# Moving work between VectorE, GpSimd and ScalarE in the spectral stage of a fused block, with reordered loads

## The chip, the cores and the metric

The kernel runs on one NeuronCore of a Trainium2 chip. The metric is the device time of one execution in microseconds (us). Every run is of one core.

Engine names as the profile prints them: PE is TensorE (matmuls), PEld its weight loads, DVE is VectorE, ACT is ScalarE, POOL is GpSimd, SP is the engine that issues DMAs.

## The reference

A block with layer norm and modulation, a spectral filter, and a gated feed-forward part:

```
mod = (silu(c) @ w_mod)                     # six rows: sa, ca, ga, sb, cb, gb
h = layernorm(x) * (1 + ca) + sa            # x: 2048 x 640, bf16
X = rfft2(h) * (w_r + 1j * w_i)             # filter in the frequency domain
x = x + ga * irfft2(X)
h = layernorm(x) * (1 + cb) + sb
x = x + gb * ((silu(h @ w_gate) * (h @ w_up)) @ w_down)    # 640 -> 1728 -> 640
```

The kernel computes the Fourier transforms as matmuls with tables.

## The kernel before

There are four stages. The *front* transforms the rows (to about 40 us). The *spectral middle* walks through 21 groups of at most four spectral lines: transform, multiply with the filter, transform back. The *inverse stage* makes the 16 output tiles of the filter and the second layer norm. The *feed-forward part* takes the remaining two thirds.

Line numbers below are those of the kernel named; the change shifts them, so the product line is L490 before and L496 after.

One group in the middle goes through three functions, and all engines work on neighbouring groups at the same time.

```python
def stage_a(g):                                     # TensorE, then VectorE
    for i, l in enumerate(ls):
        nc.tensor.matmul(xps[:, i, 0:192], lhsT=B2[:, j, :], rhs=KS2, ...)      # L476
        # (last ten groups: five one-column matmuls for the modulation, L480)
    for hl in range(2):                             # two products with the filter
        nc.vector.tensor_tensor(PP[:, 1:4, hl], xv[:, :, hl], in1, ALU.mult)    # L490
    nc.vector.tensor_copy(PP[:, 0], PP[:, 1])       # L491: the first plane again

def stage_b(g, PP):                                 # 8 matmuls, then an evacuation
    nc.tensor.matmul(yps[:, i, :], lhsT=_rev(PP, ...), rhs=identb[:], ...)      # L499
    nc.scalar.copy(Y2[:, 0:n, :], yps[:, 0:n, :])                               # L502

def stage_c(g, Y2):                                 # 4 matmuls, evacuation, rotation
    nc.tensor.matmul(eps_[:, i, :], lhsT=Y2[:, i, :], rhs=Ktab[...], ...)       # L511
    if g % 8 == 7:
        nc.vector.tensor_copy(Ev, ev)                                           # L526
    else:
        nc.scalar.copy(Ev, ev)                                                  # L528
    ...
    rot(l8, l0 + 4 - l8, slice(0, 64), nc.gpsimd)   # every second group: two ops

# in the loop over the groups:
    sa_add(g + 4)                                   # GpSimd adds a constant, four times
    if g in (0, 2):
        wsum(Wv, 16 * g, 16 * g + 32, nc.vector)    # weight sums
    if g in (9, 13):                                # "RI products": scale the RI table
        nc.gpsimd.tensor_tensor(RI[:, v], RI[:, v], ga_bc[:], ALU.mult)
# ... cut: the front, the inverse stage, the feed-forward part
```

The input `B2` of groups 5 to 20 arrives by four DMA transposes. The RI table is loaded between the second and the third of them. The gate and up weights are loaded in two pieces (columns 0 to 511, then 512 to 1663), both ahead of the DMA transpose that brings the first normalized chunk to the feed-forward part.

## Time and profile before

Median 278.97 us of 4 runs (278.12 to 279.92). The profiled execution has a span of 276.7 us.

| stage | from, us | to, us | what holds it |
|---|---|---|---|
| front | 0 | 41.77, first product | several engines |
| middle | 41.77 | 71.01, end of the last product | VectorE |
| tail of the middle | 71.01 | 74.32, first burst of inverse matmuls | a chain over three engines |
| inverse stage | 74.32 | 93.63 | TensorE |
| feed-forward | 93.63 | 276.7 | TensorE |

The page of the profile names what held the end (part 4, "chain that ended last"). The shares are of the whole span:

```profile
PE 78%; DVE 9%; DMA 5%; ACT 3%; SPq 1%; issue 1%; POOL 0%; DVEq 0%; ACTq 0%
PE psum L714 20%; PE psum L717 20%; PE psum L759 19%; DVE rM L490 3%; DMA rL<-rA 3%; DMA rW<-rL 2%; PE psum L265 2%; PE psum L313 2%; PE psum L650 2%; PE psum L665 2%; PE psum L287 2%; PE psum L284 1%; DVE rM L491 1%; PE psum L704 1%; PE psum L668 1%; PE psum L303 1%
```

L714, L717 and L759 are the feed-forward part, which the change leaves alone. The 9% of VectorE are mostly the middle. The chain also passes through a DMA transpose there (`rL<-rA`, the third of the four). It did not hold the stage: it landed at 55.92 us, while VectorE was busy all along, and the first matmul that reads it started at 57.73 us, after a wait for VectorE:

```profile
46.59 9.34 DMA rL<-rA
```

```profile
57.73 0.24 PE L476 MATMUL psum<-Ktab,rL 128*128 128x192 bf16 x1 [0.54 <-DVE rM L490]
```

In the middle the groups of instructions (window 41 to 71 us) show how full VectorE is. The columns are line, engine, operation, output and input, shapes, count; busy us and mean ns of one; idle us of the engine just before them and who ended that.

```profile
L490 DVE TENSOR_TENSOR rM<-psum,rW 128x384 bf16<-128x384 f32 (+2 forms) x42 | 21.0, 539 | 0.6 <-PE psum L476 0.6
L499 PE MATMUL psum<-identb,rM 128*128 128x128 bf16 x154 | 12.4, 220 | 1.0 <-DVE rM L490 0.5 <-DVE rM L491 0.4
...
L491 DVE COPY rM<-rM 128x256 bf16<-128x256 bf16 (+2 forms) x20 | 6.8, 340 | 0.7
...
L540 POOL TENSOR_SCALAR rE<-rE 128x512 bf16<-128x512 bf16 (+1 forms) x8 | 5.0, 626 | 11.2 <-ACT rE L528 9.7 <-DVE rE L526 1.4
```

The products wait 0.6 us in all, which is their first wait, at 41.77 us. VectorE never stops after it. GpSimd stands still for 11.2 us before its rotations (L540).

Next the timeline of VectorE in the same stage: start us, duration us, engine, line, operation. "x2" merges two instructions.

```profile
60.39 0.35 DVE L491 COPY rM<-rM 128x256 bf16<-128x256 bf16 x1
60.65 1.01 DVE L490 TENSOR_TENSOR rM<-psum,rW 128x384 bf16<-128x384 f32 x2
61.70 1.18 DVE L491 COPY rM<-rM 128x256 bf16<-128x256 bf16 x1
62.79 1.01 DVE L490 TENSOR_TENSOR rM<-psum,rW 128x384 bf16<-128x384 f32 x2
63.84 0.23 DVE L491 COPY rM<-rM 128x256 bf16<-128x256 bf16 x1
```

The same copy takes 0.23 us at 63.84 and 1.18 us at 61.70. GpSimd at that moment:

```profile
60.04 0.62 POOL L540 TENSOR_SCALAR rE<-rE 128x512 bf16<-128x512 bf16 x1 [1.30 <-ACT rE L528]
...
61.38 1.40 POOL L574 TENSOR_TENSOR rH<-rH,ga_bc 128x640 bf16<-128x640 bf16 x1
```

The 1.18 us copy starts in the shadow of a 1.40 us RI product on GpSimd, and it ends at 62.88 us, just after that product (62.79 us). Where the timelines of both engines were read (this kernel, the copies alone on GpSimd, and parts of the two weight sum runs), each of the eleven copies on VectorE that took more than 0.30 us, 0.35 to 1.23 us long, ended 0.04 to 0.08 us after an operation of GpSimd. By these ends the copy was held until GpSimd was done, rather than slowed; "stretched" means this below. Not every operation held one: at 51.08 us a copy kept its 0.23 us and ended while a 0.31 us add ran on GpSimd. The products of VectorE do not change their pace (1.01 or 1.02 us for each merged pair of full size in this kernel, whatever GpSimd does).

### The profile page before, as it was taken

To read this page: it belongs to the slowest core of one execution; us is meant where nothing else is said; L and a number is where in the kernel's file an instruction comes from. 1 tells how busy PE (TensorE), PEld (TensorE's weight loads), DVE (VectorE), ACT (ScalarE), POOL (GpSimd) and SP (SyncE) were. 2 spreads that over 40 slices of the span, in tenths; PEclk is the share of its full clock that TensorE was granted. 3 is DMA by queue.
4 is the path that set the end of the run, shared out by engine and by line. 5 is a ranking of instruction groups with operands and counts; after the bars stand their busy time and mean duration, and the time that the engine had idled before them with its cause. 6 is when DMAs were issued, how large, how long until landed. Compare 5 with 4: busy or idle time off the path is not lost.

```text
span 276.7 us, 5481 instructions
## 1 busy us (share of the span) xinstructions
PE 263.9 (95%) x2202; PEld 179.3 (65%) x2202; DVE 153.9 (56%) x371; ACT 111.6 (40%) x206; POOL 46.7 (17%) x90
## 2 busy tenths in 40 slices
PE   8899989888799999999999999999999999999995
PEld 3688768787589887644446754445764444778873
DVE  0577969999688789338634227654223633323422
ACT  2588657876777772143222022323004223103310
POOL 4277742474410002000200000200000100000000
PEclk9999999999999999999999999999999999999999
DMA  7999999999993000610050110050011020011001
GB/s 243 370 301 287 325 353 205 303 285 368 241 388 78 7 1 0 121 33 1 2 95 0 50 56 1 0 96 1 24 51 33 0 50 0 25 35 43 1 2 47
DMA packets 40952, 31.30 MB, mean 113 GB/s; under 512 B 20831, under 2 KB 37342, under 8 KB 40542
## 3 DMA queue, kind: packets, MB, share of 16 engines
q1 hardware_dynamic: 40924, 30.94, 38.6%
q8 instruction: 17, 0.28, 0.4%
q14 instruction: 9, 0.07, 0.1%
q10 hardware_dynamic: 2, 0.00, 0.0%
HBM read 23.37 MB, written 4.72 MB: 101 GB/s over the span
## 4 chain that ended last, share of the span: by engine, by line
PE 78%; DVE 9%; DMA 5%; ACT 3%; SPq 1%; issue 1%; POOL 0%; DVEq 0%; ACTq 0%
PE psum L714 20%; PE psum L717 20%; PE psum L759 19%; DVE rM L490 3%; DMA rL<-rA 3%; DMA rW<-rL 2%; PE psum L265 2%; PE psum L313 2%; PE psum L650 2%; PE psum L665 2%; PE psum L287 2%; PE psum L284 1%; DVE rM L491 1%; PE psum L704 1%; PE psum L668 1%; PE psum L303 1%
## 5 line engine op out<-in xcount | busy, mean ns | idle before, releaser
L714 PE MATMUL psum<-rW 128*128 128x512 bf16 (+1 forms) x325 | 66.9, 336 | 0.0
L717 PE MATMUL psum<-rW 128*128 128x512 bf16 (+1 forms) x325 | 66.9, 336 | 0.0
L720 ACT ACTIVATE rE<-psum 128x512 f32<-128x512 f32 (+1 forms) x65 | 33.3, 512 | 68.4 <-PE psum L714 68.3
L717 PEld LDWEIGHTS <-rW 128*128 128x128 bf16 x325 | 31.8, 98 | 24.5
L714 PEld LDWEIGHTS <-rW 128*128 128x128 bf16 x325 | 31.8, 98 | 24.5
L721 DVE TENSOR_TENSOR rX<-psum,rE 128x512 bf16<-128x512 f32 x26 | 17.9, 688 | 30.0 <-PE psum L717 28.5
L764 DVE TENSOR_TENSOR rE<-psum,rM 128x640 bf16<-128x640 f32 x15 | 12.4, 824 | 38.3 <-PE psum L759 38.3
L721 DVE TENSOR_TENSOR rE<-psum,rE 128x256 bf16<-128x256 f32 (+1 forms) x39 | 19.9, 511 | 24.6 <-PE psum L717 22.6
L759 PE MATMUL psum<-rA,rE 128*128 128x320 bf16 x224 | 31.2, 299 | 0.7 <-DVE rA L727 0.6
L759 PE MATMUL psum<-rA,rX 128*128 128x320 bf16 x224 | 30.8, 299 | 0.0
L759 PEld LDWEIGHTS <-rE 128*128 128x128 bf16 x224 | 21.9, 98 | 9.6 <-issue 0.6
L759 PEld LDWEIGHTS <-rX 128*128 128x128 bf16 x224 | 21.9, 98 | 8.8
L623 POOL TENSOR_TENSOR rstd<-rstd,mhalf 128x4 f32<-128x4 f32 (+1 forms) x5 | 4.4, 885 | 136.6 <-DVE rstd L619 107.3
L706 ACT ACTIVATE rE<-psum 64x512 f32<-64x512 f32 (+1 forms) x5 | 2.5, 506 | 48.1 <-PE psum L704 48.1
L490 DVE TENSOR_TENSOR rM<-psum,rW 128x384 bf16<-128x384 f32 (+2 forms) x42 | 21.0, 539 | 0.6 <-PE psum L476 0.6
L337 DVE SCALAR_TENSOR_TENSOR rE<-rE,msum,psum 128x648 bf16<-128x648 f32 x16 | 14.2, 889 | 4.1 <-PE psum L287 3.6
L502 ACT CAST rL<-psum 128x512 bf16<-128x512 f32 (+2 forms) x21 | 12.3, 586 | 7.3 <-PE psum L499 6.8
L670 DVE TENSOR_TENSOR rM<-psum,rX 128x640 f32<-128x640 f32 x16 | 12.9, 815 | 3.4 <-PE psum L668 3.4
L499 PE MATMUL psum<-identb,rM 128*128 128x128 bf16 x162 | 13.1, 220 | 1.3 <-DVE rM L490 0.8
L306 ACT COPY rE<-psum 128x640 bf16<-128x640 bf16 x16 | 10.9, 693 | 8.0 <-PE psum L304 8.0
L655 ACT CAST rL<-psum 128x640 bf16<-128x640 f32 x16 | 10.9, 690 | 4.6 <-PE psum L652 3.4
L352 ACT CAST rA<-psum 128x648 bf16<-128x648 f32 x15 | 10.5, 700 | 5.1 <-PE psum L349 3.9
(127 smaller groups left out, 361.7 us busy)
## 6 DMA issues: line engine op xcount, KB each, us to landing
rM<-in_w_mod_dram SPq DMA_DIRECT2D x4, 800.0 KB, 6.3
out_dram<-rE SPq DMA_DIRECT2D x16, 160.0 KB, 1.8
rA<-in_B_w_down_dram SPq DMA_DIRECT2D x1, 2080.0 KB, 13.2
rX<-in_A_x_dram SPq DMA_DIRECT2D x3, 640.0 KB, 8.2
rM<-in_w_mod_dram SPq DMA_DIRECT2D x1, 1600.0 KB, 7.9
rW<-in_B_w_gate_dram SPq DMA_DIRECT2D x1, 1440.0 KB
rW<-in_B_w_up_dram SPq DMA_DIRECT2D x1, 1440.0 KB, 13.5
rE<-tab_G SPq DMA_DIRECT2D x4, 256.0 KB, 8.4
```

The source lines that it names most:

```text
L306: nc.scalar.copy(hT[:, :, 0:128], xt)
L337: nc.vector.scalar_tensor_tensor(Z[:].rearrange("p (h r) n -> p h (r n)", h=2), Cb[:].rearrange("p (h r) n -> p h (r n)", h=2), msum[:, t: ...
L490: nc.vector.tensor_tensor(PP[:, 1:4, hl], xv[:, :, hl], in1, ALU.mult)
L499: nc.tensor.matmul(yps[:, i, :], lhsT=_rev(PP, 128 * n * ps + i, [[n, 128]]), rhs=identb[:], start=(ps == 1 and i == 0), stop=(ps == 0 and ...
L502: nc.scalar.copy(Y2[:, 0:n, :], yps[:, 0:n, :])
L670: nc.vector.tensor_tensor(x1[:, t, :].rearrange("p (m h r) -> p m h r", h=2, r=2), ops[:, :, 0:320].rearrange("p h (r m) -> p m h r", r=2) ...
L714: nc.tensor.matmul(gu[:, 0, 0:N], lhsT=Wgu[:, 0, c5, fc * 128:(fc + 1) * 128], rhs=h2T[:, :, c5, :], start=(c5 == 0), stop=(c5 == NC5 - 1))
L717: nc.tensor.matmul(gu[:, 1, 0:N], lhsT=Wgu[:, 1, c5, fc * 128:(fc + 1) * 128], rhs=h2T[:, :, c5, :], start=(c5 == 0), stop=(c5 == NC5 - 1))
L720: nc.scalar.activation(sg[:], gu[:, 0, 0:N], ACT.Silu)
L721: nc.vector.tensor_tensor(AT[:, fc, :], gu[:, 1, 0:N], sg[:], ALU.mult)
L759: nc.tensor.matmul(ops4[:, h, 0:320], lhsT=AT[:, fc, tl * 128:(tl + 1) * 128], rhs=Wd_sb[:, fc, h * 320:(h + 1) * 320], start=(fc == 0), s ...
L764: nc.vector.tensor_tensor(xo[:].rearrange("p (h m) -> p h m", h=2), ops4[:, :, 0:320], x1[:, t, :].rearrange("p (h m) -> p h m", h=2), ALU ...
```

## The change

Its intent is to spread the middle evenly over the engines. The core of the diff, with cuts:

```diff
-            nc.vector.tensor_copy(PP[:, 0], PP[:, 1])
+            if g % 4 == 0:
+                nc.vector.tensor_copy(PP[:, 0], PP[:, 1])
+            else:
+                nc.gpsimd.tensor_scalar(PP[:, 0], PP[:, 1], 1.0, 1.0, ALU.mult, ALU.mult)
...
-                nc.gpsimd.tensor_tensor(B2b[:, :nb, 0:1], B2b[:, :nb, 0:1], SA[...], ALU.add)
+                nc.vector.tensor_tensor(B2b[:, :nb, 0:1], B2b[:, :nb, 0:1], SA[...], ALU.add)
...
-            if g in (9, 13):
-                v = (g - 9) // 4
-                nc.gpsimd.tensor_tensor(RI[:, v], RI[:, v], ga_bc[:], ALU.mult)
+            if g + 3 == NG:
+                ...
+                for v in (1, 0):
+                    nc.vector.tensor_tensor(RI[:, v], RI[:, v], ga_bc[:], ALU.mult)
...
+            elif g < NG - 4:                  # two groups evacuated in one go
+                n = len(groups[g]) + 4
+                nc.scalar.copy(ep_views(l0, n), banks(6, 2, [8, 128])[:, 8 - n:8, :]...)
+                rot(l0, n, slice(0, 64), nc.gpsimd)
...
+            if slot == 0:                     # evacuation and constant in one operation
+                nc.vector.tensor_tensor(B2[:], tp[:, :n, :], SAx[:], ALU.add)
...
-        nc.sync.dma_start(RI[:], RI_dram)     # between the DMA transposes
         nc.sync.dma_start(wm_r[:, :, 1:3, :], wm_m[:, :, 1:3, :])
...
         nc.sync.dma_start(Htab[:], H_dram)
+        nc.sync.dma_start(RI[:], RI_dram)
...
-    for lo, hi in ((0, 512), (512, 1664)):
+    wgu_dma(0, 512)
+    wgu_dma(512, 1024)
...
             if t == 5:
                 ln2_tr(0)
+                wgu_dma(1024, 1664)           # behind the first chunk's transpose
```

Cut: the last four groups are evacuated and rotated in pieces by ScalarE and VectorE; two accumulations of the front use other PSUM banks; one weight sum of the front moves a tile earlier, the one of group 0 to before the loop and the one of group 2 to group 4; the last matmuls of a group are delayed so that two groups go together, and their input Y2 gets four buffers instead of two; the modulation rows are evacuated in another order.

More of the change, by code (lines that the diff above doesn't have):

```diff
@@ L177, in adaln_block_kernel @@
     SA = const.tile([P, NL], F32, name="SA")
+    SAx = gb_bc[:, 0:512].rearrange("p (l k) -> p l k", l=4)
     x_sb = rX.cut(0, [NT, D])
@@ L342, in s1 @@
         def s1(t, Z, Gs):
-            aps = banks(6, 2, [2, 512]) if t < NT - 1 else zbank(t - 1)
+            aps = banks(0 if t in (13, 15) else 6, 2, [2, 512])
             zr, zi = Z[:, :, 0:81], Z[:, :, 81:162]
@@ L369, in adaln_block_kernel @@
         nc.gpsimd.memset(SL[:], 0.0)
+        nc.gpsimd.memset(SAx[:], 0.0)
         nc.gpsimd.tensor_copy(sc_rep[:], sc_f[:].unsqueeze(2).to_broadcast([P, NC5, 128]))
@@ L399, in adaln_block_kernel @@
                 gscale(t)
-            if t in (9, 11, 13, 15):
-                wsum(Wn, 8 * t - 72, 8 * t - 56, nc.vector)
+            if t in (9, 11, 13, 14):
+                i = (9, 11, 13, 14).index(t)
+                wsum(Wn, 16 * i, 16 * i + 16, nc.vector)
             if t == NT - 1:
-                mps = psum[:, 0, 0:NC5]
+                mps = psum[:, 2, 480:480 + NC5]
                 mod_cols(mps, wm_sa, True)
@@ L409, in adaln_block_kernel @@
                                   src.unsqueeze(2).unsqueeze(3).to_broadcast([P, 4, 2, NT]))
-        sps = psum[:, 1, 0:NL]
+        sps = psum[:, 2, 0:NL]
         for i in range(16):
@@ L415, in adaln_block_kernel @@
         wsum(Wn, 64, 81, nc.vector)
+        nc.vector.tensor_scalar_mul(SAx[:, :, 0], sps[:, 64:68], float(P))
+        nc.vector.tensor_scalar_mul(SA[:], sps, float(P))
         wsum(Wv, 64, 81, nc.vector)
-        nc.vector.tensor_scalar_mul(SA[:], sps, float(P))
     Em = rE.cut(0, [2, 64, 128])
@@ L451, in t2_pe @@
             B2 = (rM.cut(38400 + 1024 * slot, [n, 128]) if slot < 2 else rM.cut(10240 + 1024 * (slot - 2), [n, 128]))
-            nc.scalar.copy(B2[:], tp[:, :n, :])
-            eng = nc.vector if slot == 0 else nc.gpsimd
-            eng.tensor_tensor(B2[:, 0:4, 0:1], B2[:, 0:4, 0:1], SA[:, ls[0]:ls[0] + 4].unsqueeze(2), ALU.add)
+            if slot == 0:
+                nc.vector.tensor_tensor(B2[:], tp[:, :n, :], SAx[:], ALU.add)
+            else:
+                nc.scalar.copy(B2[:], tp[:, :n, :])
+                nc.gpsimd.tensor_tensor(B2[:, 0:4, 0:1], B2[:, 0:4, 0:1], SA[:, ls[0]:ls[0] + 4].unsqueeze(2), ALU.add)
             if n > 4:
-                eng.tensor_tensor(B2[:, 4:6, 0:1], B2[:, 4:6, 0:1], SA[:, 0:81:80].unsqueeze(2), ALU.add)
+                nc.gpsimd.tensor_tensor(B2[:, 4:6, 0:1], B2[:, 4:6, 0:1], SA[:, 0:81:80].unsqueeze(2), ALU.add)
             for i, l in enumerate(ls):
@@ L467, in sa_add @@
                 seen.add(l0)
-                nc.gpsimd.tensor_tensor(B2b[:, :nb, 0:1], B2b[:, :nb, 0:1], SA[:, l0:l0 + nb].unsqueeze(2), ALU.add)
+                nc.vector.tensor_tensor(B2b[:, :nb, 0:1], B2b[:, :nb, 0:1], SA[:, l0:l0 + nb].unsqueeze(2), ALU.add)
         def stage_a(g):
@@ L490, in stage_a @@
                 nc.vector.tensor_tensor(PP[:, 1:4, hl], xv[:, :, hl], in1, ALU.mult)
-            nc.vector.tensor_copy(PP[:, 0], PP[:, 1])
+            if g % 4 == 0:
+                nc.vector.tensor_copy(PP[:, 0], PP[:, 1])
+            else:
+                nc.gpsimd.tensor_scalar(PP[:, 0], PP[:, 1], 1.0, 1.0, ALU.mult, ALU.mult)
             return PP
@@ L500, in stage_b, with ep_views, stage_c, evac @@
                                      start=(ps == 1 and i == 0), stop=(ps == 0 and i == n - 1))
-            Y2 = rL.cut(12288 + 1024 * (g % 2), [4, 128])
+            Y2 = rL.cut(12288 + 1024 * (g % 4), [4, 128])
             nc.scalar.copy(Y2[:, 0:n, :], yps[:, 0:n, :])
             return Y2
-        def stage_c(g, Y2):
-            ls = groups[g]
-            n, l0 = len(ls), ls[0]
-            eps_ = banks(6 + g % 2, 1, [4, 128])
-            for i, l in enumerate(ls):
-                kv = {0: 1, 80: 2}.get(l, 0)
-                nc.tensor.matmul(eps_[:, i, :], lhsT=Y2[:, i, :], rhs=Ktab[:, 128 * kv:128 * kv + 128], start=True, stop=True)
-            ev = eps_[:, :n, :].rearrange("p i q -> p q i")
+        def ep_views(l0, n):
+            if l0 < 64:
+                return Em[:, 0].rearrange("p q (c j) -> p (q c) j", c=2)[:, :, l0:l0 + n]
+            return Er[:, 0, :, :, l0 - 64:l0 - 64 + n].rearrange("p q c j -> p (q c) j")
+        units = [(0, 1), (2, 3), (4,)] + [(g, g + 1) for g in range(5, NG - 2, 2)] + [(NG - 2,), (NG - 1,)]
+        def stage_c(u):
+            for g in units[u]:
+                ls = groups[g]
+                n, l0 = len(ls), ls[0]
+                eps_ = banks({NG - 2: 1, NG - 1: 3}.get(g, 6 + (l0 // 4) % 2), 1, [4, 128])
+                Y2 = Y2s.pop(g)
+                for i, l in enumerate(ls):
+                    kv = {0: 1, 80: 2}.get(l, 0)
+                    nc.tensor.matmul(eps_[:, i + 4 - n if l0 else i, :], lhsT=Y2[:, i, :], rhs=Ktab[:, 128 * kv:128 * kv + 128],
+                                     start=True, stop=True)
+        def evac(u):
+            g, l0 = units[u][0], groups[units[u][0]][0]
             if l0 == 0:
@@ L515, in stage_c @@
                     nc.scalar.copy(Em[:, :, :, 64 * i].rearrange("p v q -> p q v"),
-                                   eps_[:, i, :].rearrange("p (q v) -> p q v", v=2))
+                                   banks(6, 1, [4, 128])[:, i, :].rearrange("p (q v) -> p q v", v=2))
+            elif g == NG - 2:
+                nc.vector.tensor_copy(ep_views(l0, 4), banks(1, 1, [4, 128]).rearrange("p i q -> p q i"))
             elif g == NG - 1:
+                nc.scalar.copy(ep_views(l0 - 12, 8)[:, 0:64], banks(6, 2, [8, 128]).rearrange("p i q -> p q i")[:, 0:64])
                 for h in range(2):
-                    nc.vector.tensor_copy(Em[:, 0].rearrange("p q (c j) -> p (q c) j", c=2)[:, 64 * h:64 * h + 64, l0:l0 + n],
-                                          ev[:, 64 * h:64 * h + 64])
-                    rot(l0, n, slice(32 * h, 32 * h + 32), nc.vector)
-            else:
-                Ev = (Em[:, 0].rearrange("p q (c j) -> p (q c) j", c=2)[:, :, l0:l0 + n] if l0 < 64 else
-                      Er[:, 0, :, :, l0 - 64:l0 - 64 + n].rearrange("p q c j -> p (q c) j"))
-                if g % 8 == 7:
-                    nc.vector.tensor_copy(Ev, ev)
-                else:
-                    nc.scalar.copy(Ev, ev)
-                if g == NG - 2:
-                    rot(l0, n, slice(0, 64), nc.gpsimd)
-                elif l0 % 8 == 4:
-                    l8 = max(l0 - 4, 1)
-                    rot(l8, l0 + 4 - l8, slice(0, 64), nc.gpsimd)
+                    hq = slice(64 * h, 64 * h + 64)
+                    nc.scalar.copy(ep_views(l0, 4)[:, hq], banks(3, 1, [4, 128]).rearrange("p i q -> p q i")[:, hq])
+            elif g < NG - 4:
+                n = len(groups[g]) + 4
+                nc.scalar.copy(ep_views(l0, n), banks(6, 2, [8, 128])[:, 8 - n:8, :].rearrange("p i q -> p q i"))
+                rot(l0, n, slice(0, 64), nc.gpsimd)
         def rot(l0, n, qs, eng):
@@ L541, in rot, with mod_bc, ga_mod @@
             eng.tensor_scalar(E1[:, :, 0, :], E0[:, :, 1, :], -1.0, 1.0, ALU.mult, ALU.mult)
-        def mod_bc(i, bank):
-            h = i % 2
+        def mod_bc(j, lo, bank):
             gps_ = psum[:, bank, 0:320]
             for k in range(NC5):
-                nc.tensor.matmul(gps_, lhsT=sc_rep[:, k, :], rhs=wm_r[:, k, 3 * (i // 2), 320 * h:320 * (h + 1)],
-                                 start=(k == 0), stop=(k == NC5 - 1))
-            if i < 2:
-                nc.scalar.copy(ga_bc[:, :, 80 * h:80 * h + 80], gps_.rearrange("p (m r) -> p r m", r=4))
-            else:
-                nc.scalar.copy(gb_bc[:, 320 * h:320 * h + 320], gps_)
+                nc.tensor.matmul(gps_, lhsT=sc_rep[:, k, :], rhs=wm_r[:, k, j, lo:lo + 320], start=(k == 0), stop=(k == NC5 - 1))
+            return gps_
+        def ga_mod(lo, bank):
+            nc.scalar.copy(ga_bc[:, :, lo // 4:lo // 4 + 80], mod_bc(0, lo, bank).rearrange("p (m r) -> p r m", r=4))
         PPs, Y2s = {}, {}
@@ L559, in adaln_block_kernel @@
         PPs[1] = stage_a(1)
+        wsum(Wv, 0, 32, nc.vector)
         t2_pe(3)
-        mod_bc(0, 6)
+        ga_mod(0, 6)
         for g in range(NG + 1):
@@ L564, in adaln_block_kernel @@
                 PPs[g + 2] = stage_a(g + 2)
+            if g + 3 == NG:
+                nc.vector.tensor_copy(modcols[:, 2, :], psum[:, 2, 192:197])
+                nc.vector.tensor_copy(modcols[:, 3, :], psum[:, 4, 192:197])
+                nc.vector.tensor_scalar_add(one_p_cb[:], modcols[:, 3, :], 1.0)
+                for v in (1, 0):
+                    nc.vector.tensor_tensor(RI[:, v], RI[:, v], ga_bc[:], ALU.mult)
+            if g == NG - 2:
+                nc.vector.tensor_copy(gb_bc[:, 0:320], mod_bc(3, 0, 5))
+            if g == 4:
+                wsum(Wv, 32, 64, nc.vector)
             sa_add(g + 4)
@@ L567, in adaln_block_kernel @@
                 Y2s[g] = stage_b(g, PPs.pop(g))
-            if g in (0, 2):
-                wsum(Wv, 16 * g, 16 * g + 32, nc.vector)
             if g == 0:
-                mod_bc(1, 7)
-            if g in (9, 13):
-                v = (g - 9) // 4
-                nc.gpsimd.tensor_tensor(RI[:, v], RI[:, v], ga_bc[:], ALU.mult)
-            if g == NG - 1:
-                mod_bc(2, 5)
-                nc.vector.tensor_copy(modcols[:, 2, :], psum[:, 2, 192:197])
-                nc.vector.tensor_copy(modcols[:, 3, :], psum[:, 4, 192:197])
-                nc.vector.tensor_scalar_add(one_p_cb[:], modcols[:, 3, :], 1.0)
-            if g >= 1:
-                stage_c(g - 1, Y2s.pop(g - 1))
-        mod_bc(3, 3)
+                ga_mod(320, 7)
+            for u, gs in enumerate(units):
+                if gs[-1] + (1 if gs[0] >= NG - 2 else 2) == g:
+                    stage_c(u)
+                    evac(u)
+        nc.scalar.copy(gb_bc[:, 320:640], mod_bc(3, 320, 4))
+        rot(48, 16, slice(0, 8), nc.vector)
+        rot(48, 16, slice(8, 32), nc.vector)
+        nc.vector.tensor_copy(ep_views(48, 8)[:, 64:128], banks(6, 2, [8, 128]).rearrange("p i q -> p q i")[:, 64:128])
+        rot(48, 16, slice(32, 64), nc.vector)
     nc.gpsimd.memset(Wd_sb[64:128, 13, :], 0.0)
@@ L590, in adaln_block_kernel, with wgu_dma @@
     nc.sync.dma_start(Wp13[:, :, 64:128], B_w_up[:, 1664:1728].rearrange("(c5 dp) f -> dp c5 f", dp=P))
-    for lo, hi in ((0, 512), (512, 1664)):
+    def wgu_dma(lo, hi):
         nc.sync.dma_start(Wgu[:, 0, :, lo:hi], B_w_gate[:, lo:hi].rearrange("(c5 dp) f -> dp c5 f", dp=P))
         nc.sync.dma_start(Wgu[:, 1, :, lo:hi], B_w_up[:, lo:hi].rearrange("(c5 dp) f -> dp c5 f", dp=P))
+    wgu_dma(0, 512)
+    wgu_dma(512, 1024)
     x1 = rM.cut(0, [NT, D], F32)
```

## The prediction

> **What bounds the kernel now.** From 93.6 us to the end of the 276.7 us span the chain of waits is almost only matmuls of the feed-forward part (lines 714, 717, 759: 20, 20 and 19% of the span). The change leaves them alone. It works on the spectral middle, from the first transposes (39.9 us) to the first inverse-transform matmul (74.3 us in the timeline). There the chain is VectorE: from the first product (line 490, 41.8 us) to the end of the last one (71.0 us) it never idles for more than 0.2 us. For 21 groups of spectral lines it issues two products (0.47 us apart) and one copy (line 491, usually 0.23 us), about 1.18 us a group. TensorE needs about 1.0 us a group, 1.13 us with the modulation columns, by the timeline's start times. GpSimd is mostly waiting.
>
> Several copies of line 491 last 0.35 to 1.18 us, each while GpSimd runs; I add up 2.3 us of such stretching. [...] the products, with one PSUM input, keep 0.505 us throughout.
>
> **What changes there.** VectorE loses 15 of 21 copies (3.5 us unstretched, and most of the 2.3 us), two 0.69 us evacuations, and the two-step tail of the last group. It gains two scalings of the RI table (about 0.45 us each, from line 727's time), four small adds, [...] and two evacuations of its own. GpSimd takes the copies at 0.48 us each (line 326, same 128x256 shape) and loses two 1.4 us RI products and the adds. ScalarE evacuates two groups in one go: about 0.91 us instead of twice 0.48.
>
> So all four engines end near 0.95 to 1.1 us a group. GpSimd's copy now lies between product and the next matmuls, and it can stand behind two 0.6 us rotations. I laid the four in-order queues out with these durations (an estimate). For the kernel before it gives 71.0 us for the first inverse matmul, 3.3 us early, about what the stretched copies and the tail explain. For the kernel after it gives 68.2 us; I add 0.8 us for remaining contention: 69.0 against 74.3. Before the middle I expect 0.2 us at most: ScalarE's last evacuations (to 39.9 us) end no sooner.
>
> **What follows.** The inverse stage stays bound by TensorE (1.11 us a tile), the feed-forward part too, so nearly all of the 5.3 us should reach the end. DMA is over 0.9 busy until 83 us, so weights won't arrive earlier; the split of the weight load lets the transpose of the first normalized chunk land (estimated at 84 us) just before its use (85 us).
>
> **Prediction: 273.7 us, range 272.2 to 276.2. Faster by over 2%: 0.42; within 2%: 0.55; slower: 0.03.**
>
> **Signs.** Right: products 1.0 to 1.1 us apart per group; line of the copy mostly on GpSimd at about 0.5 us; first inverse matmul near 69 us; feed-forward starts near 88.4 us and lasts 183 us as before. Wrong if: TensorE waits for GpSimd's copy by more than 2 us in total; copies on GpSimd take over 0.6 us; VectorE waits for a DMA transpose or for RI; or TensorE idles before the feed-forward part because the transposed chunk lands late.

One term on VectorE, a modulation row's evacuation (128 x 320), took 0.48 us in the kernel after. The sum was laid out with that term: 68.2 us, plus 0.8 us by judgement, makes 69.0 us for the first inverse matmul, 5.3 us less than 74.3 us. That each engine works in program order was the assumption for the layout; in the trace VectorE's products and copies do follow the order of the groups (41.77 to 71.04 us). ScalarE's 0.91 us for 1024 elements was an estimate: in the kernel before, two evacuations of 512 start 0.48 us apart (46.22 and 46.70 us); in the kernel after, the chain has one of 1024 at 65.42 us with 0.91 us.

## The result, and the profile after

The kernel after takes 273.54 us (median of 11 runs, 272.84 to 275.65), against 279.0 us for the kernel before (16 runs, 278.12 to 282.1). The ratio is 0.9794, with a 95% interval of 0.9763 to 0.9825. Ratios here are the mean time of one kernel's fast runs over that of the other's of the same rounds, so they differ a little from the ratio of the medians. Executions over 1.5% slower than the fastest of the same kernel are left out of the means. Since 2% lies inside the interval, "faster by over 2%" stays unclear.

Where the time went, from the timelines of the two profiled executions (spans 276.7 and 271.0 us). The inverse stage ends here with the end of its last matmul, 0.16 us after the feed-forward part's first one has started:

| stretch | before, us | after, us | difference |
|---|---|---|---|
| to the first product | 41.77 | 41.14 | -0.63 |
| first product to end of the last | 29.24 | 24.29 | -4.95 |
| from there to the first burst of inverse matmuls | 3.31 | 3.40 | +0.09 |
| inverse stage | 19.31 | 19.25 | -0.06 |
| feed-forward part | 183.07 | 182.92 | -0.15 |

The chain that ended last, on the page of the kernel after:

```profile
PE 84%; ACT 4%; DMA 4%; DVE 4%; issue 1%; POOL 1%; SPq 1%; ACTq 0%; DVEq 0%
```

VectorE's share fell from 9% to 4%, TensorE's rose. The groups of instructions in the middle (window 41 to 66 us):

```profile
L496 DVE TENSOR_TENSOR rM<-psum,rW 128x384 bf16<-128x384 f32 (+2 forms) x42 | 20.7, 540 | 1.4 <-PE psum L482 1.2
L508 PE MATMUL psum<-identb,rM 128*128 128x128 bf16 x152 | 12.2, 220 | 0.9 <-POOL rM L500 0.9
...
L500 POOL TENSOR_SCALAR rM<-rM 128x256 bf16<-128x256 bf16 (+1 forms) x15 | 6.3, 426 | 5.3 <-DVE rM L496 4.3 <-DVE rL L474 1.0
...
L555 POOL TENSOR_SCALAR rE<-rE 128x512 bf16<-128x512 bf16 (+1 forms) x7 | 4.3, 611 | 2.9 <-ACT rE L547 2.9
```

Fifteen copies now stand on GpSimd at a mean of 426 ns, and TensorE waited for one of them, 0.9 us. The products now wait for TensorE (1.2 us), which they hardly did before.

The busy time of each engine per stretch shows the change of hands. The columns are stretch, length, then busy us (and instructions) of PE, PEld, DVE, ACT and POOL, the granted clock, the DMA share and GB/s. First the kernel before:

```profile
46.00:53.00 7.00, 5.62 (x79) 4.94 (x77) 6.83 (x19) 5.83 (x13) 3.25 (x5) 1.00 0.97 301
53.00:60.00 7.00, 6.19 (x103) 5.68 (x101) 6.83 (x17) 5.33 (x10) 3.92 (x6) 1.00 1.10 222
60.00:66.00 6.00, 5.32 (x90) 4.87 (x89) 5.86 (x13) 4.22 (x8) 3.91 (x6) 1.00 1.04 387
```

Then the kernel after:

```profile
46.00:53.00 7.00, 5.77 (x84) 5.40 (x84) 6.84 (x19) 5.51 (x11) 4.35 (x8) 1.00 1.03 272
53.00:60.00 7.00, 6.84 (x126) 6.76 (x126) 6.57 (x16) 6.35 (x11) 4.78 (x10) 1.00 1.10 278
60.00:66.00 6.00, 6.00 (x106) 5.75 (x104) 5.65 (x17) 5.20 (x8) 4.52 (x10) 1.00 1.03 380
```

Before, VectorE is busy 6.83 of 7 us in 46 to 53 and in 53 to 60 us. After, it still is in the first of these, but from 60 to 66 us TensorE is busy all the time (6.00 of 6). From 53.7 to 64.8 us the chain of waits of the kernel after is TensorE alone, with 0.9 us a group and another 0.45 us for every second one, so 1.125 us a group. One group of it, with the L529 matmuls that come every second time (start us, duration us, engine, output, line):

```profile
56.87 0.08 PE psum L482
56.95 0.10 PE psum L486 x5
57.05 0.27 PE psum L482 x3
57.33 0.45 PE psum L508 x8
57.77 0.45 PE psum L529 x8
```

### The profile page after: what moved, and what is told of

It is laid out like the page before. It is cut to its first block, busy times and chain, and to the rows that moved or that the text cites. A ratio compares the mean times of both kernels' runs of the same rounds, so it can differ in the third digit from the quotient of the medians.

```text
span 271.0 us, 5494 instructions
## 1 busy us (share of the span) xinstructions
PE 261.0 (96%) x2202; PEld 178.5 (66%) x2202; DVE 151.1 (56%) x364; ACT 110.3 (41%) x198; POOL 47.7 (18%) x96
## 4 chain that ended last, share of the span: by engine, by line
PE 84%; ACT 4%; DMA 4%; DVE 4%; issue 1%; POOL 1%; SPq 1%; ACTq 0%; DVEq 0%
PE psum L738 21%; PE psum L741 20%; PE psum L783 20%; PE psum L508 2%; PE psum L673 2%; PE psum L482 2%; DMA rW<-rL 2%; DMA rX<-in_A_x_dram 2%; PE psum L688 2%; PE psum L314 2%; PE psum L288 2%; PE psum L285 2%; PE psum L691 1%; PE psum L728 1%; PE psum L304 1%
## 5 line engine op out<-in xcount | busy, mean ns | idle before, releaser
L745 DVE TENSOR_TENSOR rE<-psum,rE 128x256 bf16<-128x256 f32 (+1 forms) x39 | 19.9, 511 | 24.6 <-PE psum L741 22.6
```

Source lines behind the costliest of these rows:

```text
L745: nc.vector.tensor_tensor(AT[:, fc, :], gu[:, 1, 0:N], sg[:], ALU.mult)
```

## The experiments

Each experiment is one edit to one of the two kernels. Profiles are compared by four marks: the start of the first product, the end of the last, the first burst of inverse matmuls, and the first feed-forward matmul (93.5 us in the kernel before, 87.9 us in the kernel after). The time from the first product to the inverse burst, "the middle", is free of what happens in the front. It repeats well: the kernel after was profiled three times, and the middle took 27.69, 27.67 and 27.69 us. The kernel before and each variant were profiled once, and the calls ran on different chips.

The medians are less steady. Apart from the 305.9 us run, TensorE's mean granted clock was 0.993 or 0.994 in twelve runs and 0.997 or more in all others whose clock is on record; in each call these twelve are the slowest runs of their kernel. The only profile among them (first look at the old weight pieces, 0.993) has one dip: 0.62 and 0.53 in two stretches of 2 us. By an estimate from these figures that is 1.7 us of lost clock, or 0.6% of the span, which is about what the mean lacks.

| kernel | middle, us | first feed-forward matmul, us |
|---|---|---|
| before | 32.55 | 93.5 |
| before, copies to GpSimd | 29.82 | 90.8 |
| before, three moves | 31.01 | 92.0 |
| before, no rotations | 29.97 | 92.0 |
| after (three profiles) | 27.67 to 27.69 | 87.9 to 88.5 |
| after, all copies on VectorE | 30.72 | 91.0 |
| after, all copies on GpSimd | 27.77 | 88.6 |
| after, single evacuations | 28.11 | 89.0 |
| after, weight sum late | 28.47 | 88.9 |
| after, one weight load, first look (clock low from 42 to 46 us) | 28.86 | 91.4 |
| after, one weight load, second look | 27.70 | 89.9 |

The theory: VectorE was the limit of the middle, and the change pays because it takes copies, and the work that stretches them, off it, until TensorE is the limit of the second half. The rivals: another part of the change (merged evacuations, moved products, load order) made the gain; or the long copies have another cause than GpSimd.

### All copies back on VectorE

```diff
-            if g % 4 == 0:
+            if True:
                 nc.vector.tensor_copy(PP[:, 0], PP[:, 1])
```

> The kernel after, with all 21 first-plane copies back on VectorE, nothing else undone. Theory (the gain is VectorE's relief): 15 copies of 0.23 us come back, and some are stretched by GpSimd's rotations again; end of the last product at 68.5 to 70 us instead of 65.4, the run 3 to 5 us slower than the kernel after (276.5 to 278.5). Rival (the merged evacuations, the moved products and the DMA order made most of the gain): at most 1.5 us slower than the kernel after.

Measured: 276.43 us (4 runs), ratio to before 0.9868 (0.9807 to 0.9929). The products end at 68.42 us, the feed-forward part starts at 91.0 us, 3.1 us later than in the kernel after. The copies on VectorE in the middle:

```profile
L498 DVE COPY rM<-rM 128x256 bf16<-128x256 bf16 (+2 forms) x21 | 5.5, 261 | 0.7
```

The theory's ranges were missed by 0.1 us at their low end (68.42 for 68.5 to 70, 276.43 for 276.5 to 278.5), and the rival (1.5 us at most) is out. 4.1 us more of copies (5.48 against 1.35 in the traces) cost 3.0 us at the last product; about half of the rest are waits for TensorE that fell away (0.6 us in all instead of 1.2). The copies are a little over half of the gain, not all of it.

### Only the copies moved, in the kernel before

```diff
-            nc.vector.tensor_copy(PP[:, 0], PP[:, 1])
+            if g % 4 == 0:
+                nc.vector.tensor_copy(PP[:, 0], PP[:, 1])
+            else:
+                nc.gpsimd.tensor_scalar(PP[:, 0], PP[:, 1], 1.0, 1.0, ALU.mult, ALU.mult)
```

> The kernel before, with only the copies moved: every fourth stays on VectorE, the others go to GpSimd. Theory (relief of VectorE): 3 to 4.5 us faster than before, although GpSimd still has two 1.4 us RI products. Rival (GpSimd is then too busy, so the copies alone gain nothing without the rest): within 1 us of before, with TensorE waiting for GpSimd's copy by 3 us or more in total.

Measured: 275.88 us against 280.43 us (4 and 7 runs), ratio 0.9848 (0.9788 to 0.9907). By the profile the feed-forward part starts at 90.8 us, 2.7 us earlier than before. The kernel before was slow and spread (279.04 to 282.05, three of the seven with a low mean clock), so the ratio flatters; the profile is the safer reading, and by it the gain lies just under the 3 to 4.5 us expected. The rival is out: TensorE waited 0.3 us for GpSimd's copies. The copies alone bring about half of the gain. What they did not bring: TensorE waited 2.3 us for GpSimd's constant adds, which now share GpSimd with the copies, and two copies left on VectorE were long:

```profile
57.46 1.23 DVE L492 COPY rM<-rM 128x256 bf16<-128x256 bf16 x1
...
62.58 1.16 DVE L492 COPY rM<-rM 128x256 bf16<-128x256 bf16 x1
```

GpSimd's two RI products run at 57.20 and 62.26 us, 1.4 us each.

### The kernel before without the rotations (wrong result)

```diff
-                if g == NG - 2:
-                    rot(l0, n, slice(0, 64), nc.gpsimd)
-                elif l0 % 8 == 4:
-                    ...
-                    rot(l8, l0 + 4 - l8, slice(0, 64), nc.gpsimd)
...
-    lhsT=Em[:, v, 4 * t + r, :]      # and the same for Er
+    lhsT=Em[:, 0, 4 * t + r, :]
```

> The kernel before without GpSimd's rotations; wrong result on purpose (the inverse stage reads the unrotated plane twice). If GpSimd's work stretches VectorE's copies: the four that stood beside rotations alone fall back to 0.23 us, those beside the two RI products stay long; mean of the 21 copies from 0.335 to about 0.28 us, last product about 1 us earlier, total 0.8 to 1.5 us faster than before. Rival (the long copies have another cause): mean stays at 0.33 us, last product within 0.3 us of 71.0.

Measured: 277.12 us against 279.73 us, ratio 0.9918 (0.9856 to 0.9981). The result still passed the comparison with the reference, though the kernel does not compute it: the comparison does not notice that the rotated plane is missing, so for the other variants too a pass says little about this part. The copies on VectorE:

```profile
L491 DVE COPY rM<-rM 128x256 bf16<-128x256 bf16 (+2 forms) x21 | 5.2, 246 | 0.7
```

The mean fell from 335 ns (all 21 copies, 7.0 us) to 246 ns (5.2 us), and first product to last product end from 29.24 to 27.42 us. Both are about 1.8 us less: VectorE got back what GpSimd's work had cost it. By the traces 1.4 us of this stood beside rotations; the other 0.5 us is the copy that stood beside an RI product before, 0.67 us long here instead of 1.18. The rest of the shorter middle lies in the tail, where the inverse matmuls no longer wait for any rotation. Only that copy, at 62.09 us, stayed long. The rival is out. The total fell by more than expected: 2.3 us by the ratio (0.5 to 4.0 by its interval) for 0.8 to 1.5 us; the tail, which was not in the estimate, gave 0.8 us.

### The remaining six copies on GpSimd too

```diff
-            if g % 4 == 0:
+            if False:
```

> The kernel after, with the remaining 6 copies on GpSimd too. If TensorE is the limit of the second half of this stage (1.13 us a group), 6 x 0.23 us less on VectorE gains nothing: within 0.5 us of the kernel after. If VectorE is still the limit: 1 to 1.4 us faster. If GpSimd is at its limit (about 1.03 us a group): 0.5 to 2 us slower, with longer waits of TensorE for GpSimd.

Measured: 274.04 us (4 runs), ratio 0.9772 (0.9712 to 0.9832), not to be told from the kernel after (0.9768 and 0.9814). The middle takes 27.77 us, as in the kernel after (27.69). Less work on VectorE gained nothing. That alone does not show that VectorE has slack: the 1.35 us of copies that it lost came back as 1.3 us of waits for GpSimd's copies (L500), and TensorE waited 1.3 us for them instead of 0.9 us.

```profile
L496 DVE TENSOR_TENSOR rM<-psum,rW 128x384 bf16<-128x384 f32 (+2 forms) x42 | 20.5, 542 | 2.8 <-POOL rM L500 1.3 <-PE psum L482 1.3
```

```profile
PE psum L508 <- POOL rM L500: 1.3, 2, 0.9
```

That TensorE holds the second half rests on the chain of waits shown above, not on this run.

### Each group evacuated by itself

```diff
-                nc.scalar.copy(ep_views(l0, n), banks(6, 2, [8, 128])[:, 8 - n:8, :]...)
+                for b, m, o in ((6, n - 4, 8 - n), (7, 4, 0)):
+                    nc.scalar.copy(ep_views(l0 + (n - 4) * (b - 6), m), banks(b, 1, ...)[:, o:o + m, :]...)
```

> The kernel after, with each pair of groups evacuated by two ScalarE copies of 512 elements instead of one of 1024. By the durations read (0.91 us against twice 0.48 us) ScalarE gets 0.05 us more per pair and stays below TensorE's pace: within 0.5 us of the kernel after. Rival (the merged evacuation carries a good part of the gain): 1 us or more slower.

Measured: 273.93 us (6 runs), 0.9800 (0.9758 to 0.9842), beside 273.32 us and 0.9768 for the kernel after. The middle took 28.11 us instead of 27.67 us. That is 0.4 us, a small part at best, as expected. The edit splits the ScalarE operation alone: the pairing of groups, the four buffers and the new tail stay, and were not measured by themselves.

### The weights in the old two pieces (twice)

```diff
     wgu_dma(0, 512)
-    wgu_dma(512, 1024)
+    wgu_dma(512, 1664)
...
-                wgu_dma(1024, 1664)
```

> The kernel after, with the gate and up weights loaded in the old two pieces, so that 2.9 MB more or less stand in the queue before the first transposed chunk. Theory (the split keeps the transpose from queueing): the chunk lands after 86 us instead of before 85, ScalarE waits for it, and the feed-forward part starts 1 to 3 us later than 88.1 us. Rival (the queue is idle by then, the split is idle decoration): no change, within 0.3 us.

> The weight load in the old two pieces again, because in the first look an early wait for the flipped filter (1.4 us) and a lower granted clock hid its size. Theory: from the first inverse matmul to the feed-forward part 0.5 to 2 us longer than in the kernel after (19.1 us), with ScalarE waiting for the transposed chunk; total 0.5 to 2 us slower than the yardstick beside it. Rival: the 2.5 us of the first look were the early wait alone, and the total is within 0.3 us.

Measured: 276.07 us in the first look (4 runs) and 274.91 us in the second (6 runs), beside 274.00 us for the kernel after in the second (five fast runs). The ratios there are 0.9856 (0.9830 to 0.9882) and 0.9814 (0.9785 to 0.9844). Who waited on ScalarE between 70 and 97 us in the second look (waiter, releaser, us in total, times, longest):

```profile
ACT rW L665 <- DMA rW<-rL: 0.7, 1, 0.7
```

The chunk's transpose needs 7.0 us to land instead of 5.1, because 1.6 MB more weights (two pieces of 640 x 640 in bf16; not 2.9 MB, as expected) stand before it. First inverse burst to feed-forward part: 20.0 and 19.9 us in the two looks, against 19.1 us. So the split is worth 0.8 to 0.9 us, and without it one sixth of the gain would have been lost to the DMA queue. The first look lost another 1.4 us early, to a wait for the flipped filter, and 1.2 us in the middle (28.86 us), where the clock dipped; neither is the split's.

### The weight sum later (meant as an improvement)

```diff
-            if g == 4:
-                wsum(Wv, 32, 64, nc.vector)
+            if g in (9, 13):
+                wsum(Wv, 4 * g - 4, 4 * g + 12, nc.vector)
```

> The kernel after, with the 32-column weight sum at group 4 (1.00 us on VectorE, beside a rotation stretched to 1.05 us on GpSimd) split into two 16-column sums at groups 9 and 13, where TensorE is the limit. If VectorE's bursts are what still holds the first half of the stage: TensorE's 0.9 us wait for GpSimd's copy near 50 us goes, first inverse matmul 0.6 to 1.2 us earlier, total 0.5 to 1.2 us faster than the kernel after. Rival (the second half has no slack on VectorE either): within 0.3 us of it.

> The kernel after, unchanged, as the yardstick for the runs beside it: 273 to 274.5 us, first inverse matmul near 68.8 us, feed-forward part from near 88 us. Both theories expect the same of it.

Measured: 274.39 us (6 runs) beside 273.32 us. It is slower, and both theories missed. The wait near 50 us shrank from 0.9 to 0.5 us, but groups 9 and 13 are also where VectorE adds the constant that the next matmuls need:

```profile
59.96 0.68 DVE L362 TENSOR_TENSOR rW<-rW 128x512 bf16<-128x512 bf16 x1
60.57 0.63 DVE L474 TENSOR_TENSOR rM<-rM,SA 128x16 bf16<-128x16 bf16 x1
```

```profile
61.25 0.26 PE L482 MATMUL psum<-Ktab,rM 128*128 128x192 bf16 x1 [0.47 <-DVE rM L474]
```

The sum delayed the add, the add took 0.63 us (one at 50.06 us took 0.22; another, at 55.47 us, took 0.57 and ended 0.07 us after a rotation on GpSimd), and TensorE waited 0.47 us. First inverse burst: 69.85 instead of 68.90 us. The middle took 28.47 us, 0.8 us more. The likely mistake is the place, directly in front of an operation that TensorE needs; so the run does not settle whether VectorE has slack elsewhere in the second half.

### The weight sum on GpSimd (meant as an improvement)

```diff
+        wsum(Wv, 32, 48, nc.gpsimd)           # after the third group's transposes
...
-            if g == 4:
-                wsum(Wv, 32, 64, nc.vector)
+            if g == 2:
+                wsum(Wv, 48, 64, nc.gpsimd)
```

> The kernel after, with the 32-column weight sum of group 4 (1.00 us on VectorE) done on GpSimd instead, in two 16-column pieces placed where GpSimd sat idle (near 42.2 and 46.6 us; about 1.15 us each, estimated from its 1.4 us for 640 elements). Theory (VectorE holds the first half of the stage, groups 0 to 8, TensorE the second): TensorE's 0.9 us wait near 50 us shrinks, first inverse matmul 0.5 to 1 us earlier, total 0.5 to 1 us faster than the kernel after. Rival (GpSimd's extra 2.3 us delays its own copies just as much): within 0.3 us or slower.

> The kernel after, unchanged, as the yardstick beside the next two: 273 to 274.5 us, feed-forward part from near 88 us.

Measured: 274.40 us beside 274.00 us (five fast runs each), ratios 0.9839 (0.9812 to 0.9866) and 0.9814 (0.9785 to 0.9844): no gain. Its profile fell into the slow state (span 304.1 us, granted clock 0.852), so its times are not compared with others. Inside that profile one thing is plain, and the lower clock does not show in the two engines concerned: pairs of full-size products on VectorE take 1.01 or 1.02 us, the copy at 55.70 us 0.23 us and GpSimd's rotations from 53.15 us on 0.62 us, all as in the kernel after.

```profile
45.34 1.15 POOL L362 TENSOR_TENSOR rW<-rW 128x512 bf16<-128x512 bf16 x1
...
50.71 1.16 POOL L362 TENSOR_TENSOR rW<-rW 128x512 bf16<-128x512 bf16 x1
```

```profile
45.33 1.23 DVE L498 COPY rM<-rM 128x256 bf16<-128x256 bf16 x1
...
51.10 0.81 DVE L498 COPY rM<-rM 128x128 bf16<-128x128 bf16 x1
```

The first two lines are GpSimd's sums, the last two VectorE's copies that started beside them: 1.23 and 0.81 us instead of 0.23 and 0.20 us. VectorE gave away a 1.00 us sum and got 1.61 us of stretching back.

### Three moves, in the kernel before

The copies as above, plus:

```diff
-            if g in (9, 13): ...  nc.gpsimd.tensor_tensor(RI[:, v], RI[:, v], ga_bc[:], ALU.mult)
+            if g + 3 == NG:
+                for v in (1, 0):
+                    nc.vector.tensor_tensor(RI[:, v], RI[:, v], ga_bc[:], ALU.mult)
-                nc.gpsimd.tensor_tensor(B2b[:, :nb, 0:1], ...)
+                nc.vector.tensor_tensor(B2b[:, :nb, 0:1], ...)
```

> The kernel before with three moves between VectorE and GpSimd and nothing else of the change: 15 of the 21 copies to GpSimd, both RI products and the later constant adds to VectorE. With the copies alone the two copies beside an RI product took 1.23 and 1.16 us and TensorE waited 2.3 us for GpSimd's adds. Theory (what remained of the gain was those two): both go, last product end near 66.3 us instead of 68.1, total 1.2 to 2.2 us faster than with the copies alone, so 4 to 5 us faster than before. Rival (the rest of the gain needs the merged evacuations, the new tail or the moved loads): at most 0.5 us faster than with the copies alone.

Measured: 276.59 us against 278.78 us, ratio 0.9912 (0.9883 to 0.9941); 2.2 us faster than before, and not faster than with the copies alone. The theory is out. The rival's bound (at most 0.5 us faster than with the copies alone) holds, but it did not foresee a longer middle, 31.01 against 29.82 us. What happened there:

```profile
58.75 0.23 DVE L468 TENSOR_TENSOR rL<-rL,SA 128x16 bf16<-128x16 bf16 x1 [2.03 <-DMA rL<-rA]
```

```profile
55.11 0.28 PE L480 MATMUL psum<-sc_col,rM 128*128 128x1 bf16 x5 [0.96 <-DMA rM<-in_w_mod_dram]
...
59.04 0.26 PE L476 MATMUL psum<-Ktab,rL 128*128 128x192 bf16 x1 [1.59 <-DVE rL L468]
```

With the old load order, TensorE waited 0.96 us for modulation weights, and VectorE waited 2.03 us for the third DMA transpose. The engines had become faster than the loads that feed them. In the three profiles of the kernel after, which loads RI behind the transposes, no engine waits for a transpose. So the moved RI load may be what lets the moved products and adds pay. That is argued, not shown: the same transposes also ran without such a wait in the profile with the copies alone, loads were late elsewhere in this profile (0.7 us for the flipped filter), and the load order was never changed by itself.

## Why the prediction was right

- **Total.** 273.7 us predicted, 273.54 us measured, inside 272.2 to 276.2.
- **VectorE bound the middle, and its relief is the gain.** Shown from both sides for a good half of it: the copies alone shorten the middle by 2.7 us, taking them back lengthens it by 3.0 us, of 4.9 us in all. What brought the other 1.9 to 2.2 us stays open.
- **2.3 us of copies stretched by GpSimd.** Shown for 1.8 us: the mean copy fell from 335 to 246 ns without rotations. (The 0.505 us of the prediction is half of a merged pair, 1.01 us, whose two products overlap; one product takes 0.54 to 0.56 us, beside GpSimd or not.)
- **The copies on GpSimd.** 0.48 us was assumed, from an operation of the same shape; they took 0.43 us. TensorE waited 0.9 us for them; the sign of failure was 2 us.
- **The middle.** The estimate of 69.0 us for the first inverse matmul compares with 68.83 us. The terms were less exact than their sum, so the close hit is partly luck: the front came 0.4 us earlier than allowed and the middle took 0.3 us more than the estimate leaves for it, and 0.8 us of the 69.0 us had been added by judgement. The front gave 0.63 us where 0.2 us at most was allowed; the wrong step is the sentence that ScalarE's last evacuations end no sooner. They ended 0.3 us sooner, and the evacuation with the constant in one VectorE operation saved about as much again. The middle itself took 1.16 us a group (24.29 / 21), where 0.95 to 1.1 was stated; TensorE alone takes 1.125 us a group in the second half.
- **The tail.** The prediction counts the loss of "the two-step tail of the last group" as relief. It is not: last product to first inverse burst takes 3.40 us now and 3.31 us before. The chain of waits has ScalarE there, with copies back to back from 64.84 us to 68.35 us.
- **What follows.** The feed-forward part started at 88.08 us (88.4 predicted) and lasts as before. The transposed chunk landed at 83.9 us (78.80 + 5.1; 84 predicted) and was used at 84.98 us (85). Undoing the split showed that this margin was real: 0.8 to 0.9 us.
- **Left open.** The moved RI products and adds, the one-step constant, the pairing of groups, the four buffers of Y2 and the load order were not each measured alone. With all copies back on VectorE, these together still shorten the middle by 1.8 us (32.55 to 30.72). The merged evacuations are worth about 0.4 us, no more than the spread of the runs.

## What to carry to other kernels

Before moving work from VectorE to GpSimd, look not only at what VectorE saves but at which of its remaining operations stand beside the moved one. Here a copy of bf16 data on VectorE was held (1.23 us instead of 0.23 at worst); a product with one operand in PSUM was not (0.54 to 0.56 us throughout). When a stage gets faster, look whether the loads that feed it and the next one still arrive in time, and put first in the DMA queue what is used first: here that was worth 0.8 to 0.9 us for the transposed chunk. And when all engines of a stage are nearly full, do not expect much of a further move between them: three such attempts here gained nothing, and no version ran that beats the kernel after.

## What else the traces show

- **VectorE beside GpSimd.** A copy of 0.23 us on VectorE took up to 1.23 us, until the GpSimd operation beside it had ended. VectorE's own 32-column sum, both inputs in SBUF, took 0.68 us alone. Beside a rotation it took 1.00 us in the kernel after, and that rotation 1.05 us; in the kernel before the sum kept its 0.68 us and the rotation took 1.15 us, where a rotation alone takes 0.62 us. The full-size products with one PSUM input took 0.54 to 0.56 us each in both kernels.
- **The same work on the two engines.** The copy takes 0.23 us on VectorE and 0.41 us on GpSimd. For the RI product, with two bf16 inputs, the gap is wider: 0.49 us (kernel after) against 1.40 us (kernel before), 2.9 times.
- **A gap of TensorE and the granted clock.** In the first look with the weights in two pieces a gap of 1.76 us was followed by a granted clock of 0.62 and 0.53 in the next two stretches of 2 us (lines below); in the kernel before without rotations a wait of 1.6 us at the same place left the clock at 1.00. What decided between the two is not shown.

```profile
42.05 0.50 PE L482 MATMUL psum<-Ktab,rM 128*128 128x192 bf16 x4 [1.76 <-DVE rM L457]
...
44.02 1.54 PE L561 MATMUL psum<-rM,sc_rep 128*128 128x320 bf16 x5
```

```profile
42.00:44.00 2.00, 1.95 (x18) 1.90 (x19) 1.37 (x4) 0.59 (x1) 0.21 (x1) 0.62 0.57 125
44.00:46.00 2.00, 2.00 (x13) 1.36 (x11) 1.44 (x3) 1.21 (x2) 1.06 (x3) 0.53 1.20 228
```

  Five 320-column matmuls take 1.54 us there; in the kernel after they take 0.84 us.
- **A load that lands late.** The wait for the flipped filter before the first product varied from none to 1.7 us between profiles with the same loads in the front (none in the kernel after, 1.68 us in the kernel before without rotations); part of the spread of the runs may come from there and part from the clock dips, but that was not tested.
